# Four edits to a single-core attention and experts kernel: where the weights' low words are made, first matmuls on TensorE, when one block's keys and values are loaded, and where the bias tables come from

## The chip, the cores and the metric

The kernel runs on one core of a Trainium2 chip. The metric is the device time of one execution in microseconds (us), lower is better. The times are medians of several runs; beside them stands one execution that was profiled, with a time and a span of its own. Engines are named as the profile names them: PE (TensorE, matrix multiply), PEld (its weight loads), DVE (VectorE), ACT (ScalarE), POOL (GpSimd), SP (SyncE, which here only issues DMAs). PSUM is the memory that PE writes to, SBUF the working memory.

## The reference

Three layers follow one another, all in float32. There are 4 x 576 = 2304 tokens of width 512.

```python
# 1. attention, B, H, S, D = 4, 8, 576, 64, window 128
scores = np.matmul(q, k.transpose(0, 1, 3, 2)) / np.sqrt(D)
bias = slopes[:, None, None] * (-np.abs(rel))      # slopes[h] = 2.0 ** -(h + 1)
mask = (rel >= 0) & (rel < 128)
scores = np.where(mask, scores + bias, -1e9)
attn = softmax(scores)                              # row maximum taken off, sum + 1e-9
x = heads_joined(np.matmul(attn, v))                # (2304, 512)
# 2. dense layer, w_in 512 x 2048, w_out 2048 x 512
h = x @ w_in
x = (h - np.tanh(h)) @ w_out
# 3. eight experts, one per token
idx = argmax(normalised(x) @ normalised(expert_emb).T / tau)
out[idx == e] = gate * (np.maximum(x[idx == e] @ w1[e], 0) @ w2[e])
```

## The kernel before

Products that need float32 exactness are made of two words: a matrix is rounded to a high word (a cast, usually by ACT) and a low word (the matrix less its high word, a subtraction with two inputs by DVE or POOL), and PE multiplies high by high, high by low and low by high.

The work is cut into tasks. Each task has one engine, or a choice of engines with a cost for each (a dictionary such as `{"DVE": 0.72, "POOL": 1.32}`), a due time, and the things that it reads and writes. A planner (`Plan.order`) walks through the tasks with these costs: of the tasks that are ready it takes the one that can start first, and of those that can start together the one with the smallest due time. The order that comes out is the order of the instructions on each engine; the engines then run in order, and wait for each other only where data demand it. `port=True` tells the planner that such a task doesn't start on DVE while POOL is at work. SP's DMAs are one in-order queue: an issue that waits for its buffer holds all the issues behind it.

Attention goes over 18 blocks of 128 tokens, each in four quarters of two heads (`quarter`). In a quarter PE makes the scores (L485 in blocks 0 to 3, which use float32 keys and queries in one piece; L491 later, with two words, `khl` and `qst`). DVE adds the bias and takes the maximum (`soft`, L513), which reads the table `bias` of that head. ACT takes the exponential (`exp`, L527), PE transposes (`tr_pe`, L548), ACT or DVE copies the result out (L552), and PE multiplies it by the values (`pv_f`, L562). `x_out` transposes the finished block for the dense layer (L664, and L671 and L672 split it into words in `xT`). Blocks 0 and 1 have to be finished before the first step of the dense layer (`step`, L712 and L736) can start. The two score banks are reused: the next scores into a bank wait for the exponential that reads it.

The bias tables are made on the chip before: SP loads one float32 table (`tmp`, L251), and `consts` multiplies it by the slope of each head (L255), two heads on DVE and six on POOL; POOL also casts the triangle `tri` that the routing needs (L258).

Blocks 0 to 3 take keys and queries from their own loads (`qk_early`, L415 and L420). Block 4 needs the keys and values of block 3 also in the later form, so `qk_half` and `v_half` run for block 3 as well: SP loads `stk` (L375; one buffer, so the second half waits until the first is used) and `vst` (L443), ACT casts (L381), and POOL or DVE subtracts (L385).

The dense layer's weights (`weight`, L335 and on) are 32 loads of 512 KB that DVE and ACT unpack (L339, L342, L347, L351). After seven of the nine groups of two blocks, the routing (`route`) decides on the expert of each token: a chain of small DVE instructions (L826, L830, `chain` with L847 to L852) whose result `oh` PE multiplies by `tri` (`pos`, L862). In the same stretch the experts' weights begin to arrive: `e_weight` loads a piece of 128 x 512, ACT casts it (L1080) and DVE or POOL makes the low word (L1084). There are 128 such pieces. The experts' products are L1186, L1217, L1221 and, for one tile, L1306.

Of the kernel before, what the change touches and what calls it, by code (L numbers as in the profile page):

```python
# [10 lines left out]
F32 = mybir.dt.float32  # L11
F32R = mybir.dt.float32r
F16 = mybir.dt.float16
BF16 = mybir.dt.bfloat16
# [4 lines left out]
ALU = mybir.AluOpType  # L19
# [4 lines left out]
B, H, S, D = 4, 8, 576, 64  # L24
# [15 lines left out]
NF = 4  # L40
# [7 lines left out]
WLEAD2 = 6  # L48
N0 = 1
NPX = 16  # L50
NALT = 8
NOWN = 8
NXO = 2
# [2 lines left out]
QK = 2  # L56
# [122 lines left out]
class Builder:  # L179
# [61 lines left out]
    def zero(self, P):  # L241
        for n, t in enumerate(self.wz):
            P.add({"DVE": 0.6}, lambda e, t=t: self.nc.vector.memset(t, 0), -30, w=[("wz", n)])

    def consts(self, P):
        nc, i = self.nc, self.i
        at = {}

        def tmp(e):
            at[0] = self.at.tile([128, 512], F32, tag="xr", name="tmp", bufs=1)  # L250
            nc.sync.dma_start(out=at[0][:, 0:384], in_=i["c_bias"])  # L251

        P.add({"SP": 0.55}, tmp, -20, w=[("xr", m) for m in range(4)])
        for h in range(H):
            P.add({"DVE": 0.3} if h < 2 else {"POOL": 0.88}, lambda e, h=h: self.eng(e).tensor_scalar(  # L255
                out=self.bias[:, h, :], in0=at[0][:, 0:256], scalar1=2.0 ** -(h + 1), scalar2=None, op0=ALU.mult),
                -20 + h, r=[("xr", 0)], w=[("bias", h)])
        P.add({"POOL": 0.5}, lambda e: nc.gpsimd.tensor_copy(out=self.tri, in_=at[0][:, 256:384]), -11,  # L258
              r=[("xr", 0)], w=["tri"])

    def small(self):
        nc, i = self.nc, self.i
# [194 lines left out]
    def quarter(self, P, a, due):  # L457

        nc = self.nc
        b, qd = divmod(a, 4)  # L460
        hf, qq = divmod(qd, 2)
        s, n = b % 2, (2 * b + hf) % 2
# [9 lines left out]
        bank = "acc" if a < NALT and a % 2 else "sc"  # L472
# [141 lines left out]
        for jj in range(2):  # L614
            if early:
                P.add({"PE": 0.3 if one else 0.42}, lambda e, jj=jj: scores(jj), due,
                      r=["at", ("qf", b)] + [("kf", x) for x in ([b] if one else [b, b - 1])], w=[(bank, jj)])
            else:
                P.add({"PE": 0.13 if one else 0.24}, lambda e, jj=jj: scores(jj), due,
                      r=["at"] + ks + [("kl", x, hf) for x in kv] + q, w=[(bank, jj)])  # L620
        for jj in range(2):
            P.add({"DVE": ttr}, lambda e, jj=jj: soft(jj), due, r=["at", ("bias", qd * 2 + jj)],
                  w=[(bank, jj), ("mx", jj, a % 2)])
        for jj in range(2):
            P.add({"ACT": 0.49 if one else 0.64}, lambda e, jj=jj: exp(jj), due,
                  r=["at", (bank, jj), ("mx", jj, a % 2)], w=[("p32", pb, jj), ("sm", sk, qq, jj)])
        sm = [("sm", sk, x, y) for x in range(2) for y in range(2)]
        half = [("xr", 2 * hf), ("xr", 2 * hf + 1)]
        if early:
# [3 lines left out]
                  r=["at", ("tp", a)] + ([("h", own)] if own is not None else []), w=[("pt", a % 2)],  # L633
                  free="misc" if own is None else None)
            P.add({"PE": 0.45 if one else 0.9}, pv_f, due,
                  r=["at", ("pt", a % 2)] + [("vf", x) for x in ([b] if one else [b - 1, b])], w=[("o", qq)] if qq else ["o", ("o", 0), ("o", 1)])
            if qq:
# [4 lines left out]
              w=[("ph", a % 2)], port=True)  # L642
        P.add({"POOL": 0.84, "DVE": 0.46} if one else {"POOL": 1.19, "DVE": 0.71}, s_lo, due,
              r=["at", ("p32", pb, 0), ("p32", pb, 1), ("ph", a % 2)], w=[("ph", a % 2, 1)], port=True)
        P.add({"SP": 0.7 if one else 1.2}, tr, due, late=LATE, r=["at", ("ph", a % 2), ("ph", a % 2, 1)], w=[("pt", a % 2)])
        P.add({"PE": 0.28 if one else 0.56}, pv, due,
              r=["at", ("pt", a % 2)] + [("vt", x, hf, m) for x in kv for m in range(3)], w=["o"])
# [412 lines left out]
    def e_weight(self, P, e, kind, f, due):  # L1060

        nc, i = self.nc, self.i
        ff = f + FE // 128 * (e % 2)
        n = self.nld % NST
        self.nld += 1
        key, st = (kind, ff), ("est", n)
        v = {}
        w1, w2 = [i[w].rearrange("e k f -> (e k) f") for w in ("w1", "w2")]

        def load(_):  # L1070
            t = v["x"] = self.ex.tile([128, 512], F32, tag=f"est{n}", name="est")
            if kind == "i":
                half, k = divmod(f, KD)
                nc.sync.dma_start(out=t, in_=w1[bass.ds(self.at_row[e][0] + k * 128, 128), half * 512:(half + 1) * 512])
            else:
                nc.sync.dma_start(out=t, in_=w2[bass.ds(self.at_row[e][1] + f * 128, 128), :])

        def hi(_):
            t = self.w[key] = self.wp.tile([128, 2, 512], F32R, tag=f"w{kind}{ff}", name=f"e{kind}{ff}")
            nc.scalar.copy(out=t[:, 0, :], in_=v["x"])  # L1080

        def lo(eng):
            t = self.w[key]
            self.eng(eng).tensor_tensor(out=t[:, 1, :], in0=v["x"], in1=t[:, 0, :].bitcast(F32), op=ALU.subtract)  # L1084

        P.add({"SP": 0.73}, load, due - 4, r=["at", ("place", e)], w=[st], lag=LAG)
        P.add({"ACT": 0.65}, hi, due, r=[st], w=[(key, 0), (key, 1)])
        P.add({"DVE": 0.72, "POOL": 1.32}, lo, due, r=[st, (key, 0)], w=[(key, 1)], port=True)

    def e_rows(self, P, v, t, due):  # L1090

# [249 lines left out]
    def build(self):  # L1341
        tc, nc = self.tc, self.nc
        for n in ("kf", "qf", "vf", "sums", "oh4", "qst", "xr", "acc", "w"):
            setattr(self, n, {})
        self.setup()
        dp = self.pool("dr", bufs=1, space=DRAM, tilewait=False)
        self.bucket = dp.tile([ROWS, ROW], F32, name="bucket")
        self.pa = dp.tile([2 * N0, 128, DM], F32, name="pa")
        self.nw = 0
        self.sent, self.puts = [], []  # L1350
        P = Plan()
        P.add({"POOL": 2.7}, lambda e: self.small(), 0, w=["small", "cum"])
        self.zero(P)
        self.consts(P)
        self.small_loads(P, -19)
        all_f = list(range(FP))
        fa, fb = all_f[:FA], all_f[FA:]
        visits = ([(g, fa) for g in range(N0)] + [(N0, all_f)] + [(g, fb) for g in range(N0)]
                  + [(g, all_f) for g in range(N0 + 1, NG)])

        def weights(fps, due, rate):
            for x, fp in enumerate(fps):
                for kind in "io":
                    for f in (2 * fp, 2 * fp + 1):
                        self.weight(P, kind, f, due + x * rate + 1.2 * (kind == "o"))

        weights(fa, -WLEAD, WRATE)
        p, xi, seen = 0, 0, set()
        for g, fps in visits:
            sl = [xi % XR, (xi + 1) % XR]  # L1370
            xi += 2
            rate = RATE if g <= N0 else 1.0
            for n in range(2):
                b = 2 * g + n
                d0 = p - 8 * rate - (LEADM if g > N0 else LEAD) + 4 * n * rate
                if g not in seen:
                    for hf in range(2):
                        due = d0 + 2 * hf * rate
                        self.qk_half(P, b, hf, due - QK)
                        if b < NF and hf == 0:  # L1380
                            self.qk_early(P, b, due - QK - 2)
                            self.v_full(P, b, due)
                        if b >= NF - 1:
                            self.v_half(P, b, hf, due)
                        for qq in range(2):
                            self.quarter(P, 4 * b + 2 * hf + qq, due + qq * rate)
                if g not in seen:
                    self.x_out(P, b, sl[n], d0 + 4 * rate)
                    if b == 0:
                        self.emb(P, 0)  # L1390
            if g == N0:
                weights(fb, p + len(fa) - WLEAD2, WRATE2)
            for fp in fps:
                self.step(P, p, g, fp, sl, fp == fps[0], fp == fps[-1])
                for e in range(E):
                    if p == PAD + e // PADN:
                        self.pad(P, e, p)
                p += 1
            if g < N0 and g not in seen:
                self.spill(P, p - 1, g, sl)  # L1400
            else:
                if g == NG - 1:
                    self.moe2(P, p, lambda: self.route(P, g, sl, p))
                else:
                    self.route(P, g, sl, p + 1)
                if g == NG - 3:
                    self.choose(P, p + 2)
                    self.space(P, p + 2)
            seen.add(g)
        with tc.manual_schedule():  # L1410
            for fn, e in P.order({"misc": 1}):
                fn(e)
        self.overflow()
        while self.open:
            k = list(self.open)[-1]
            self.close(k)
# [140 lines left out]
def layout(inputs):  # L1557
    f = np.float32
# [6 lines left out]
    def tr(x):  # L1565
# [18 lines left out]
        "emb": np.ascontiguousarray(inputs["moe2_expert_emb"]),  # L1584
        "w1": np.ascontiguousarray(inputs["moe2_w1"]),
        "w2": np.ascontiguousarray(inputs["moe2_w2"]),
        "c_bias": np.concatenate([cur, prev, r < c], axis=1).astype(f),
        "c_con": np.concatenate([
            np.eye(128, dtype=f), row(np.arange(E, dtype=f) - E), row(np.arange(E, dtype=f) * NT),
            (np.arange(NB)[None, :] * 128 + r).astype(f), row(np.asarray(inputs["moe2_tau"]).reshape(1))], axis=1),  # L1590
# [16 lines left out]
```

## Time and profile before

| | |
|---|---|
| Median of 3 runs | 781.98 us (780.95 to 782.5) |
| Profiled execution, its own time | 785.27 us |
| Profiled execution, span from first to last instruction | 783.4 us |
| PE busy | 760.1 us, 97% of the span |
| DVE, ACT, POOL busy | 549.5, 427.9, 382.6 us |
| Mean granted clock of PE | 0.993 |

The span is told by the trace; the time of the execution is 1.9 us longer. Busy shares are averages over stages with different limits, and a busy PE need not be at its full rate, so the stages are read one by one.

### The profile page before, as it was taken

What the parts mean: (1) busy time and instruction counts of PE and PEld (TensorE: products, weight loads), DVE (VectorE), ACT (ScalarE), POOL (GpSimd) and SP (SyncE); (2) the same over time, 40 slices, a digit from 0 to 9 for tenths busy, and PEclk for the clock granted to TensorE, in tenths of its full rate; (3) what the DMA queues carried; (4) which work ended last, traced back from release to release, by engine and by line L of the source; (5) the groups of instructions that cost most, each with busy time, mean ns of one, the idle gap of its engine ahead of it and who ended that gap; (6) DMA issues with size and microseconds to landing.
All of it is one profiled execution on the core that took longest, in us unless ns stands there. A gap on an engine that the chain in (4) does not pass through costs nothing.

```text
span 783.4 us, 15248 instructions
## 1 busy us (share of the span) xinstructions
PE 760.1 (97%) x5189; PEld 678.7 (87%) x5189; DVE 549.5 (70%) x1454; ACT 427.9 (55%) x969; POOL 382.6 (49%) x378
## 2 busy tenths in 40 slices
PE   6998999999999999999999999989999999999996
PEld 4877899889998999989899998979879898888895
DVE  4888887888777688778777776887626678675420
ACT  4878776655565465555645643645235565555321
POOL 3226023674666165364744732687216577655411
PEclk9999999999999999999999999999999999999998
DMA  7996169966365353554454243764257879897100
GB/s 269 385 372 195 44 200 296 247 155 113 108 131 139 69 116 104 119 117 133 95 123 121 62 81 88 184 201 148 76 160 208 230 218 261 216 237 218 44 29 30
DMA packets 152454, 124.25 MB, mean 159 GB/s; under 512 B 115301, under 2 KB 119397, under 8 KB 152112
## 3 DMA queue, kind: packets, MB, share of 16 engines
q1 hardware_dynamic: 149344, 111.39, 53.5%
q0 software_dynamic: 3024, 11.82, 4.1%
q8 instruction: 42, 0.69, 0.4%
q14 instruction: 44, 0.36, 0.2%
HBM read 84.29 MB, written 22.06 MB: 136 GB/s over the span
## 4 chain that ended last, share of the span: by engine, by line
PE 87%; DVE 4%; issue 4%; ACT 2%; POOL 2%; DMA 1%; SPq 0%; POOLq 0%
PE h L712 25%; PE acc L736 23%; PE he L1186 12%; PE y L1221 10%; PE o L573 3%; PE sc L491 3%; PE y L1217 3%; PE of L562 2%; PE sc L485 1%; PE misc L548 1%; PE misc L664 1%; PE ht L1306 1%; DMA tmp<-in_c_bias 1%; PE misc L821 1%; DVE xA L1146 0%
## 5 line engine op out<-in xcount | busy, mean ns | idle before, releaser
L712 PE MATMUL h<-xT,wi 128*128 128x256 f32 x1728 | 227.8, 286 | 0.8 <-DVE xT L672 0.5
L712 PEld LDWEIGHTS h<-xT,wi 128*128 128x128 f32 x1728 | 219.7, 193 | 6.8 <-DVE xT L672 0.7
L736 PE MATMUL acc<-wo,gh 128*128 128x512 f32 x576 | 183.4, 400 | 0.4 <-DVE wo L351 0.4
L736 PEld LDWEIGHTS acc<-wo,gh 128*128 128x128 f32 x576 | 101.0, 190 | 16.6 <-issue 1.0
L736 PE MATMUL acc<-wo,gl 128*128 128x512 f32 x288 | 113.0, 392 | 0.0
L717 ACT ACTIVATE t<-h 128x512 f32<-128x512 f32 x72 | 43.0, 597 | 105.7 <-PE h L712 100.2
L1221 PE MATMUL y<-eo,ge 128*128 128x512 f32 x336 | 88.0, 398 | 0.2 <-ACT yo L1229 0.2
L527 ACT ACTIVATE p<-sc,mx 128x256 f32<-128x256 f32 (+1 forms) x128 | 59.0, 462 | 39.4 <-DVE mx L513 27.4
L1221 PEld LDWEIGHTS y<-eo,ge 128*128 128x128 f32 x336 | 60.1, 188 | 10.5 <-ACT yo L1229 0.4
L729 DVE TENSOR_TENSOR gl<-t,gh 128x512 fp32r<-128x512 f32 x72 | 64.4, 895 | 6.7 <-ACT gh L725 6.4
L537 POOL TENSOR_TENSOR ph<-p,ph 128x512 f16<-128x512 f32 (+1 forms) x37 | 43.9, 1187 | 51.1 <-ACT ph L532 40.5
L736 PEld LDWEIGHTS acc<-wo,gl 128*128 128x128 f32 x288 | 54.3, 189 | 12.2
L385 POOL TENSOR_TENSOR khl<-stk,khl 64x512 fp32r<-64x512 f32 x24 | 31.8, 1325 | 67.3 <-ACT khl L381 61.3
L720 DVE TENSOR_TENSOR t<-h,t 128x512 f32<-128x512 f32 x72 | 49.5, 687 | 18.5 <-ACT t L717 18.2
L1208 DVE SCALAR_TENSOR_TENSOR ge<-he,ge 128x256 fp32r<-128x256 f32 x104 | 28.8, 315 | 46.7 <-ACT ge L1202 46.3
L513 DVE CUSTOM_DVE_ANT_0 sc<-sc,bias 128x256 f32<-128x256 f32 (+1 forms) x136 | 49.6, 374 | 15.5 <-PE sc L491 9.5
L1246 POOL DMA_INDIRECT out<-yo,ix x23 | 25.0, 1089 | 69.9 <-ACT yo L1242 63.0
L1202 ACT ACTIVATE ge<-he 128x288 fp32r<-128x288 f32 (+2 forms) x56 | 23.2, 414 | 61.2 <-PE he L1186 42.5
L1186 PEld LDWEIGHTS he<-xA,ei 128*128 128x128 f32 x384 | 54.1, 189 | 2.6
L1186 PE MATMUL he<-xA,ei 128*128 128x288 f32 (+2 forms) x384 | 56.0, 296 | 0.0
L1186 PEld LDWEIGHTS he<-xT,ei 128*128 128x128 f32 x384 | 53.5, 188 | 2.2
L1186 PE MATMUL he<-xT,ei 128*128 128x288 f32 (+2 forms) x384 | 55.0, 295 | 0.0
(224 smaller groups left out, 1444.3 us busy)
## 6 DMA issues: line engine op xcount, KB each, us to landing
est<-in_w SPq DMA_DIRECT2D x128, 256.0 KB, 3.6
bucket<-in_c_pad SPq DMA_DIRECT2D x8, 1155.0 KB, 9.7
rawi<-in_w_in SPq DMA_DIRECT2D x16, 511.8 KB, 7.3
rawo<-in_w_out SPq DMA_DIRECT2D x16, 511.8 KB, 8.9
stk<-in_k SPq DMA_DIRECT2D x30, 256.0 KB, 2.8
stq<-in_q SPq DMA_DIRECT2D x28, 256.0 KB, 3.0
vst<-in_v SPq DMA_DIRECT2D x30, 128.0 KB, 2.8
xe<-bucket SPq DMA_DIRECT2D x3, 384.0 KB, 3.4
```

The source lines that it names most:

```text
L385: self.eng(e).tensor_tensor(out=k, in0=r4("k")[64:128], in1=k.bitcast(F32), op=ALU.subtract)
L513: nc.vector.tensor_tensor_reduce(out=x, in0=x, in1=self.bias[:, h, c0:c1], scale=-0.125, scalar=mx[:, 1:2] if m else 3.0e38, op0=ALU.add, ...
L527: nc.scalar.activation(out=v["p32"][:, jj * W:(jj + 1) * W], in_=x, func=AF.Exp, scale=-1.0, bias=v["mx"][jj][:, 0:1], accum_out=self.sums ...
L537: self.eng(e).tensor_tensor(out=ph[:, 2 * W:4 * W], in0=v["p32"][:, 0:2 * W], in1=ph[:, 0:2 * W], op=ALU.subtract)
L712: nc.tensor.matmul(h3(v["h"], f2), lhsT=w[:, a, k, :], rhs=xT[c][:, :, k, :], start=(k == 0 and n == 0), stop=(k == KD - 1 and n == 2))
L717: nc.scalar.activation(out=v["t"], in_=v["h"].rearrange("p a b -> p (a b)"), func=AF.Tanh)
L720: nc.vector.tensor_tensor(out=v["t"], in0=v["h"].rearrange("p a b -> p (a b)"), in1=v["t"], op=ALU.subtract)
L729: self.eng(e).tensor_tensor(out=v["gl"], in0=v["t"], in1=v["gh"].bitcast(F32), op=ALU.subtract)
L736: nc.tensor.matmul(self.acc[g, t], lhsT=v[a][:, c0:c0 + 128], rhs=self.w["o", fs[f2]][:, c, :], start=(first and f2 == 0 and n == 0), stop ...
L1186: nc.tensor.matmul(h[:, 0:N], lhsT=w[:, a, c0:c0 + 128], rhs=xT()[b][:, k, 0:N], start=(k == 0 and n == 0), stop=(k == KD - 1 and n == 2))
L1208: nc.vector.scalar_tensor_tensor(out=g[:, o:o + c1 - c0], in0=hk[f][:, c0:c1], scalar=0.0, in1=g[:, c0:c1].bitcast(F32), op0=ALU.max, op1= ...
L1221: nc.tensor.matmul(y[t], lhsT=gt(f, a)[:, (t - ts[0]) * 128:(t - ts[0] + 1) * 128], rhs=self.w["o", f0 + f][:, b, :], start=(f == 0 and n ...
```

## The change

Four things are changed.

- `warm` is new. DVE first fills a tile with ones, and PE multiplies it by itself (128 x 512, bfloat16, results not used): 7 times ahead of everything else, 8 times after the scores of quarter 0, and twice after those of quarters 1, 2 and 3. They write the PSUM bank `h0`.
- The bias tables of all eight heads are constants in bfloat16 (128 x 2048 and the triangle of 128 x 128), loaded by three DMAs of ACT's queue: heads 0 and 1, heads 2 to 7, the triangle. SP's load, the eight multiplications and the cast are gone.
- For block 3, the due times of `qk_half` and `v_half` are 3 later.
- The low words of the experts' weights (L1084 before) are made by DVE alone.

```diff
+WARM = [7, 8, 2, 2, 2]
+    def warm(self, P, n, due, r=()):
+        nc = self.nc
+        def run(e):
+            y = self.misc("h0")
+            for _ in range(n):
+                nc.tensor.matmul(y, lhsT=self.fill[:, 0:128], rhs=self.fill, start=True, stop=True)
+        def begin(e):
+            self.fill = self.m1.tile([128, 512], BF16, tag="gh0", name="fill", bufs=1)
+            nc.vector.memset(self.fill, 1.0)
+        if not r:
+            P.add({"DVE": 0.3}, begin, -40, w=[("gh", 0)])
+        P.add({"PE": 0.22 * n}, run, due, r=[("gh", 0), *r], w=[("h", 0)])
     def consts(self, P):
-            nc.sync.dma_start(out=at[0][:, 0:384], in_=i["c_bias"])
-        P.add({"SP": 0.55}, tmp, -20, w=[("xr", m) for m in range(4)])
-        for h in range(H):
-            P.add({"DVE": 0.3} if h < 2 else {"POOL": 0.88}, lambda e, h=h: self.eng(e).tensor_scalar(
-                out=self.bias[:, h, :], in0=at[0][:, 0:256], scalar1=2.0 ** -(h + 1), ...
-        P.add({"POOL": 0.5}, lambda e: nc.gpsimd.tensor_copy(out=self.tri, in_=at[0][:, 256:384]), -11, ...
+            nc.scalar.dma_start(out=self.bias[:, h0:h1, :],
+                                in_=i["c_bias"][:, h0 * 256:h1 * 256].rearrange("p (h t) -> p h t", h=h1 - h0))
+        for h0, h1 in ((0, 2), (2, H)):
+            P.add({"AQ": 3.0}, lambda e, h0=h0, h1=h1: table(e, h0, h1), -40, w=[("bias", h) for h in range(h0, h1)])
+        P.add({"AQ": 1.0}, lambda e: nc.scalar.dma_start(out=self.tri, in_=i["c_bias"][:, H * 256:]), -40, w=["tri"])
...
+        if a + 1 < len(WARM) and WARM[a + 1]:          # in quarter(), after the scores
+            self.warm(P, WARM[a + 1], -30, [(bank, 0), (bank, 1)])
...
-        P.add({"DVE": 0.72, "POOL": 1.32}, lo, due, r=[st, (key, 0)], w=[(key, 1)], port=True)
+        P.add({"DVE": 0.72}, lo, due, r=[st, (key, 0)], w=[(key, 1)], port=True)
...
+        self.warm(P, WARM[0], -40)
...
-                        self.qk_half(P, b, hf, due - QK)
+                        late = 3 if b == NF - 1 else 0
+                        self.qk_half(P, b, hf, due - QK + late)
...
-                            self.v_half(P, b, hf, due)
+                            self.v_half(P, b, hf, due + late)
```

## Rows read from the trace of the kernel before

**Rows 1.** The page: busy time by engine.

```profile
PE 760.1 (97%) x5189; PEld 678.7 (87%) x5189; DVE 549.5 (70%) x1454; ACT 427.9 (55%) x969; POOL 382.6 (49%) x378
```

**Rows 2.** PE's waits over the run: waited for, us, times, longest.

```profile
PE sc L485 <- DMA kf<-in_k: 4.2, 1, 4.2
PE misc L862 <- DVE oh L852: 3.6, 1, 3.6
PE sc L491 <- ACT p L527: 3.1, 3, 2.7
PE sc L485 <- ACT p L527: 2.3, 1, 2.3
```

**Rows 3.** Timeline, the first 7 us: start, us, engine, line, operation.

```profile
0.88 0.48 DVE L243 MEMSET xrow<- 128x512 int32 x1 [0.88 <-PEq L1599]
...
1.16 0.42 SPq L415 DMA_DIRECT2D kf<-in_k  x1
...
6.16 0.69 DVE L255 TENSOR_SCALAR bias<-tmp 128x256 bf16<-128x256 f32 x2 [4.25 <-DMA tmp<-in_c_bias]
6.22 5.48 POOL L255 TENSOR_SCALAR bias<-tmp 128x256 bf16<-128x256 f32 x6 [4.55 <-DMA tmp<-in_c_bias]
```

**Rows 4.** Timeline of PE, 8 to 22 us.

```profile
8.39 0.69 PE L548 MATMUL misc<-con,p 128*128 128x128 f32 x2
...
13.38 1.22 PE L562 MATMUL of<-vf,ptf 128*128 128x128 f32 x4
...
18.30 0.71 PE L562 MATMUL of<-vf,ptf 128*128 128x128 f32 x4
...
20.00 0.66 PE L548 MATMUL misc<-con,p32x 128*128 128x128 f32 x4
```

**Rows 5.** The chain that ended last, in order of time: start, us, work.

```profile
99.95 2.75 PE acc L736 x12
```

**Rows 6.** Stretches: length, busy PE, PEld, DVE, ACT, POOL; PEclk, DMA share, GB/s.

```profile
8.00:12.00 4.00, 4.00 (x16) 2.67 (x15) 1.72 (x10) 2.79 (x12) 3.70 (x6) 1.00 1.02 391
...
16.50:20.00 3.50, 3.50 (x20) 2.45 (x18) 2.34 (x13) 2.33 (x9) 1.27 (x1) 1.00 0.18 56
...
69.00:72.40 3.40, 3.02 (x14) 3.02 (x15) 3.18 (x9) 2.95 (x7) 1.93 (x2) 0.50 0.00 0
```

**Rows 7.** SP's queue, two neighbouring rows of its timeline.

```profile
8.41 1.78 SPq L335 DMA_DIRECT2D rawi<-in_w_in  x3
18.20 0.33 SPq L375 DMA_DIRECT2D stk<-in_k  x1
```

**Rows 8.** Stretches where the experts' weights arrive, columns as in rows 6.

```profile
500.00:510.00 10.00, 10.00 (x73) 9.02 (x72) 9.00 (x8) 7.17 (x13) 10.00 (x7) 1.00 0.52 140
510.00:520.00 10.00, 8.82 (x67) 7.85 (x65) 9.86 (x13) 5.56 (x10) 8.65 (x8) 1.00 0.76 236
...
523.00:526.40 3.40, 3.40 (x15) 3.11 (x14) 2.87 (x6) 1.10 (x2) 2.33 (x2) 0.51 0.55 178
...
640.00:680.00 40.00, 40.00 (x233) 35.62 (x232) 33.18 (x61) 24.25 (x46) 27.68 (x24) 1.00 0.82 230
```

**Rows 9.** The same for line 1084 alone: busy DVE, busy POOL.

```profile
500.00:510.00 10.00, 1.51 (x1) 8.03 (x5) 1.00 0.52 140
510.00:520.00 10.00, 3.53 (x3) 7.96 (x7) 1.00 0.76 236
...
640.00:680.00 40.00, 15.16 (x14) 14.97 (x12) 1.00 0.82 230
```

**Rows 10.** Timeline of DVE, 499 to 530 us.

```profile
499.85 1.65 DVE L1084 TENSOR_TENSOR ei<-est,ei 128x512 fp32r<-128x512 f32 x1
...
519.91 1.19 DVE L849 TENSOR_TENSOR lg<-lg,rs 128x16 f32<-128x16 f32 x1
...
521.02 0.16 DVE L850 TENSOR_TENSOR eq<-eq,con 128x16 f32<-128x16 f32 x1
...
529.90 0.69 DVE L1084 TENSOR_TENSOR eo<-est,eo 128x512 fp32r<-128x512 f32 x1
```

More of the change, by code (lines that the diff above doesn't have):

```diff
@@ L243, in zero, with table @@
             P.add({"DVE": 0.6}, lambda e, t=t: self.nc.vector.memset(t, 0), -30, w=[("wz", n)])
+    def warm(self, P, n, due, r=()):
[10 more added lines that the diff above has]
+        P.add({"PE": 0.22 * n}, run, due, r=[("gh", 0), *r], w=[("h", 0)])
     def consts(self, P):
         nc, i = self.nc, self.i
-        at = {}
-        def tmp(e):
-            at[0] = self.at.tile([128, 512], F32, tag="xr", name="tmp", bufs=1)
-            nc.sync.dma_start(out=at[0][:, 0:384], in_=i["c_bias"])
-        P.add({"SP": 0.55}, tmp, -20, w=[("xr", m) for m in range(4)])
-        for h in range(H):
-            P.add({"DVE": 0.3} if h < 2 else {"POOL": 0.88}, lambda e, h=h: self.eng(e).tensor_scalar(
[L256 to L259, printed above, removed]
+        def table(e, h0, h1):
+            nc.scalar.dma_start(out=self.bias[:, h0:h1, :],
[3 more added lines that the diff above has]
+        P.add({"AQ": 1.0}, lambda e: nc.scalar.dma_start(out=self.tri, in_=i["c_bias"][:, H * 256:]), -40, w=["tri"])
     def small(self):
@@ L1586, in layout @@
         "w2": np.ascontiguousarray(inputs["moe2_w2"]),
-        "c_bias": np.concatenate([cur, prev, r < c], axis=1).astype(f),
+        "c_bias": np.concatenate([np.concatenate([cur, prev], axis=1) * 2.0 ** -(h + 1) for h in range(H)] + [r < c],
+                                 axis=1).astype(mybir.dt.np(BF16)),
         "c_con": np.concatenate([
```

## The prediction

> **What bounds the kernel now.** I read the page first, then PE's waits, then the stages in which PE waits or runs slowly. PE is busy for 760.1 of 783.4 us [rows 1], so nearly every stage is PE's, and what can be won is PE's idle time and its time at a low rate. The waits show where: 4.2 us for the first keys, 2.3 us behind the first scores, 2.7 us at 65.5 us, and 3.6 us for `oh` in the routing [rows 2]; the rest is small, but for the tail behind the last product, which no edit touches.
>
> At the start two things hold PE up. The first bias is multiplied at 6.16 us, though the first scores could start at 4.2, and POOL needs until 11.7 for the other heads [rows 2, 3]. And PE is slow: four value products take 1.22 us at 13.38 and 0.71 us at 18.30, two transposes 0.69 us at 8.39 and four 0.66 us at 20.00 [rows 4]. The granted clock reads 1.00 there, but I go by the durations: until about 17 us PE is at 1.2 GHz, after that at 2.4. In mid-run the chain is PE without a gap, 12 products of 512 columns in 2.75 us, 0.23 each [rows 5].
>
> The first load stage is DMA's: its engines are full at 8 us (1.02), yet 0.18 busy from 16.5 to 20 [rows 6]. SP's queue shows why: after the issues that end at 10.2 it stands until 18.20 on a load of `stk`, which is block 3's keys [rows 7]. That is 3.5 x 0.82 = 2.9 us of empty DMA.
>
> In the routing DVE is the bound: 9.00 and 9.86 of 10 us [rows 8]. In the same 20 us POOL makes 12 low words of the experts' weights, 16.0 us of work [rows 9]. DVE's two-input instructions are long there: 1.65 us for a low word and 1.19 for 16 columns, against 0.69 for a low word at 529.90 and 0.16 for 16 columns at 521.02 [rows 10]. They wait for POOL.
>
> **The change, part by part.**
>
> *Bias by ACT's queue.* Removed: eight multiplications and a cast, with 5.48 us on POOL and 0.69 on DVE [rows 3]; POOL has nothing else then, so its part counts only through the heads that were late. Added: three issues on ACT, each taken at the 0.42 us of an SP issue [rows 3]; ACT has no arithmetic before 7 us, so they are hidden, and without that cover they would cost 1.3. The tables are 544 KB instead of 192 KB: 352 KB more, 0.9 us at the 391 GB/s of [rows 6]. The keys were issued at 1.16 and are there at 4.2 [rows 2, 3]; the tables issued at about 0.7 should be there between 4 and 5, a gain of 1.2 to 2.2 us for the first soft step, if they don't hold up the keys, which costs at most 544 KB / 391 = 1.4.
>
> *Ones first.* The fill is a DVE memset, done by 1.4 us if it takes the 0.48 of its neighbour [rows 3]. A warm product isn't in the trace; by the nearest row it is 0.23 us at the upper level [rows 5], so 0.46 at the lower. The first 7 end at 1.4 + 3.2 = 4.6, into the 4.2 us wait: 0.4 late. Quarter 0's scores take some 0.6. The next 8 stand in PE's in-order queue ahead of quarter 1's scores and quarter 0's transposes, which wait for them; 2.3 us of them fall into an idle stretch. They take 1.8 us at the upper level, 3.7 at the lower, then 0.6 for scores and two more ones. The transposes, now at 8.39, come at 4.6 + 0.3 + 1.8 + 0.3 + 0.5 = 7.5 if the clock is up by 4.6, at 4.6 + 0.6 + 2.8 + 0.6 + 0.5 = 9.1 if it rises half-way through the 8, at 4.6 + 0.6 + 3.7 + 0.6 + 0.9 = 10.4 if not. From there to the products at 18.30 it takes 9.9 us now, about 8.2 at the lower level. At the upper one that is 8.2 x 0.71/1.22 + 1.7 = 6.5, plus two pairs of ones 0.9: 7.4. So the mark comes at 14.9, 16.5 or, with the clock low as long as now (9.9 + 1.8 behind 10.4), 22.1: a gain of 3.4 or 1.8, or a loss of 3.8. The nearest row decides: after 3.4 us of nearly unbroken products at 0.50, PE was granted full speed at 72.4 [rows 6]. That is the middle case: **1.8 us**.
>
> The rows also show that a busy PE alone doesn't bring the level up: 4.00 of 4.00 us busy from 8 to 12 [rows 6], at the slow durations. The Trainium skill, "TensorE: Matmul & The Clock Gate", section Part 1, says that the low clock is the default and sustained matmul activity releases it. By that alone the clock would have been up by 12 us before, against the rows; for the bursts of ones it gives the middle case, 1.8.
>
> *Block 3 later.* Eight loads and casts and their subtractions move behind some of the dense weights; the first use of `khl` is at 60 us, so nothing waits for them. SP's queue no longer stands at 10 us, so the 2.9 us hole is filled, less 0.9 for the tables: the weights come 2.0 us earlier. PE doesn't wait for them before 57 us, so the gain by itself is nothing; but it lets the 1.8 of the start pass through the stage up to 70 us, where DVE unpacks weights as they land. Bounds: 0 of the 1.8 kept, or the 2.7 wait at 65.5 and the half clock behind it (3.4 x 0.50 = 1.7) gone too.
>
> The Trainium skill, "DMA: Bandwidth & Descriptors", section "Issuing engines are not separate DMA queues", says that issuing from another engine saves only issue time, as all queues share the engines. By it the tables hold up the keys by the whole 1.4 us, and the start is worth 0.4 instead of 1.8; no row here shows two queues side by side.
>
> *Low words by DVE.* In 500 to 520 us DVE runs 20 instructions, 12 of 512 columns and 8 small. Unhindered they would be 12 x 0.69 + 8 x 0.16 = 9.6 us, against 18.9 now [rows 8, 10]: 9.3 come back when POOL is still. The 12 low words cost 12 x 0.69 = 8.3. So if all stood ahead of `oh`, it would come 1 us earlier; if few do, the small chain alone (four steps of about 1.2, each cut to 0.16) gives 4. Bounds: 0, or the 3.6 wait and the half clock behind it, 3.4 x 0.49 = 1.7 [rows 2, 8], together 5.3. Some 1.3 us of low words stay ahead: **4.0 us**. POOL's other two-input work still hinders DVE.
>
> Later, DVE is at 33.2 of 40 us in its fullest stretch [rows 8]. Twelve more low words add 8.3; its own 14 return 15.16 - 14 x 0.69 = 5.5 [rows 9]. At 36 of 40 PE still has its weights in time; without that return DVE would need 41.5 and cost 1.5.
>
> **Sum:** 785.27 - 1.8 - 4.0 = 779.5 for the profiled execution. It stands 0.42% above the median, so 779.5 x 781.98 / 785.27 = **776.2 us**.
>
> **Rivals.**
> - *The wait at 65.5 goes too.* For it: the empty DMA before it is filled. Against: DVE and ACT are full there whatever loads. 2.7 + 1.7 more: about 771.5. Chance 0.17.
> - *Little arrives.* The clock rises late, or PE comes earlier to a DVE stage that ends when it did, or `oh` comes only 1 us earlier: one of the two terms is lost, or both: 778 to 782. For it: the rows of a busy, slow PE. Chance 0.23.
> - *DVE becomes the bound in the routing.* If the 12 low words go ahead of `oh` and the 9.3 don't come back, because POOL's joins and casts keep hindering DVE, the wait grows by 8.3: 781.98 - 1.8 + 8.3 = 788.5. It decides once less than 8.3 - 1.8 = 6.5 of the 9.3 returns. Against: 16.0 of POOL's 18.7 us there are the low words. Chance 0.12.
>
> **Numbers.** The forecast has 0.48: 774 to 778.5 by its own bounds. 0.2% is 1.6 us, about what a measurement of this kernel can tell from no change. Faster: 0.48 + 0.17 + half of 0.23 = 0.77; the other half of the third case is split, 0.10 the same and the rest slower with the last case, 0.13. The range reaches down to the first rival and up to the end of the second, 770 to 782.5.
>
> **What would show it.** Transposes of quarter 0 at 9 us and short from then on; no hole in the DMA share at 17 us; DVE's low words at 0.69 us and small steps at 0.16 near 520 us; no 3.6 us wait for `oh` and no half clock there. The prediction is wrong if PE's pace at 10 to 17 us is still slow, if `oh` is as late, or if the planner's new order makes a new wait of several us.

## The result and the profile after

The changed kernel takes 773.5 us (median of 6 runs, 771.67 to 777.16), against 781.78 us of the kernel before on the same chip (6 runs, 780.49 to 784.95). The ratio is 0.9896 with a 95% interval of 0.9876 to 0.9915: 1% faster, inside the range of the forecast and 2.7 us below its middle. The profiled execution took 773.47 us with a span of 771.7, 11.7 us less than the span of before; the medians differ by 8.3, since the execution of before that was profiled is slower than any of those six.

The page, busy time by engine (against [rows 1]):

```profile
PE 758.0 (98%) x5210; PEld 673.9 (87%) x5210; DVE 548.5 (71%) x1498; ACT 430.3 (56%) x971; POOL 306.1 (40%) x324
```

PE does 21 products of ones more and is still busy for 2 us less: it ran fast for more of the time. POOL lost 76.5 us and DVE gained nothing, though it took over POOL's low words. PE's waits of the whole run, the longest four (waited for, us, times, longest):

```profile
PE misc L253 <- DVE fill L257: 1.4, 1, 1.4
PE misc L835 <- DVE xT L686: 1.4, 1, 1.4
PE sc L497 <- DMA kf<-in_k: 1.1, 1, 1.1
PE h L726 <- DVE t L734: 1.0, 1, 1.0
```

The three long waits of [rows 2] are gone: behind the first scores, at 65.5 us and for `oh`. Where they stood, PE goes on. Timeline of PE at the start (start, us, engine, line, operation; L497 are scores, L560 transposes, L574 value products, L253 ones):

```profile
1.43 3.17 PE L253 MATMUL misc<-fill 128*128 128x512 bf16 x7 [1.43 <-DVE fill L257]
5.65 0.80 PE L497 MATMUL sc<-kf,qf 64*128 64x128 f32 x4 [1.05 <-DMA kf<-in_k]
6.38 3.60 PE L253 MATMUL misc<-fill 128*128 128x512 bf16 x8
9.90 0.80 PE L497 MATMUL scx<-kf,qf 64*128 64x128 f32 x4
10.63 0.60 PE L253 MATMUL misc<-fill 128*128 128x512 bf16 x2
...
11.58 0.44 PE L560 MATMUL misc<-con,p 128*128 128x128 f32 x2
...
12.81 0.61 PE L574 MATMUL of<-vf,ptf 128*128 128x128 f32 x4
```

The keys, which PE had at 4.15 us before, come at 5.65. The ones take 0.45 us each in both bursts, the pace of the lower level; at 10.6 us it changes, and the two transposes at 11.58 take 0.44 us where before they took 0.69, the four value products 0.61 where before they took 1.22 [rows 4]. The transposes of quarter 0 come 3.2 us later than before, and all behind them runs at the upper level. The trace's own records of the granted clock begin with a step up to full speed, at 10.6 us here and at 17.8 in the kernel before, which bears out the reading by durations: the 1.00 shown ahead of that step is no measurement. Stretches (length; busy PE, PEld, DVE, ACT, POOL; granted clock, DMA share, GB/s), against [rows 6, 8]:

```profile
16.00:20.00 4.00, 4.00 (x28) 2.81 (x27) 3.58 (x18) 3.22 (x12) 0.00 (x0) 1.00 1.04 410
500.00:510.00 10.00, 10.00 (x88) 9.21 (x87) 8.22 (x16) 5.53 (x11) 0.40 (x1) 1.00 0.89 228
510.00:520.00 10.00, 10.00 (x71) 9.19 (x70) 8.53 (x29) 5.23 (x11) 2.15 (x3) 1.00 0.63 207
640.00:680.00 40.00, 39.77 (x234) 35.44 (x233) 28.30 (x67) 22.38 (x43) 12.74 (x11) 1.00 0.90 242
```

The hole in the DMA at 17 us is filled: 1.04 instead of 0.18. In the routing POOL is nearly still, and DVE runs 44 instructions in 16.75 us where before it ran 20 in 18.86 (one that crosses 510 us stands in both rows). Timeline of DVE there (against [rows 10]):

```profile
509.40 0.68 DVE L1098 TENSOR_TENSOR eo<-est,eo 128x512 fp32r<-128x512 f32 x1
...
510.80 0.18 DVE L862 TENSOR_TENSOR eq<-lg,rs 128x16 f32<-128x16 f32 x1
```

A low word takes 0.68 us and a small step 0.18, as in the undisturbed rows of before.

For the rest, four marks are read from each trace: the transposes that finish block 0 and block 3 (L664 before, L678 here), the product with `oh` near 520 us (the eighth of nine in the run, the one that PE waited 3.6 us for before), and the end of the span. Each kernel's times in us:

| kernel | block 0 | block 3 | `oh` | end |
|---|---|---|---|---|
| before | 20.50 | 64.71 | 522.40 | 783.4 |
| after | 20.02 | 62.65 | 512.98 | 771.7 |
| e1 low words alone | 19.43 | 64.23 | 519.12 | 779.4 |
| e10 late loads alone | 20.29 | 63.80 | 522.84 | 784.3 |
| e9 ones alone | 16.96 | 61.99 | 520.12 | 779.8 |
| e7 bias tables alone | 23.81 | 72.64 | 525.70 | 785.6 |
| e6 ones and tables | 18.67 | 63.49 | 519.01 | 778.7 |
| e2 after, low words undone | 19.17 | 61.80 | 513.35 | 772.9 |
| e3 after, ones undone | 26.60 | 74.57 | 529.92 | 788.2 |
| e4 after, late loads undone | 18.69 | 63.53 | 518.24 | 777.6 |
| e5 after, tables undone | 17.73 | 61.84 | 513.27 | 771.7 |
| e11 first ones only | 26.56 | 74.53 | 533.90 | 794.0 |
| e8 nine and four ones | 16.37 | 58.89 | 517.89 | 781.0 |
| e12 most tables by SP | 17.71 | 65.33 | 519.67 | 781.4 |

They are marks of one execution each, and two of the profiled executions are far from typical: that of e9 lies 4.3 us above the median of e9 and that of e8 4.5 us above the median of e8, the slowest of each. The start also moves from run to run. The kernel before and e1 have the same order of instructions on every engine up to about 500 us, and so have the changed kernel and e2 up to about 495; yet block 0 ends 1.1 us earlier in e1 and 0.85 in e2, where the level rose earlier (16.2 against 17.8 us, 8.8 against 10.6). So leads of under 1 us in this table say little, and the comparisons go by the medians. By the marks the changed kernel is 2.1 us ahead at block 3, 9.4 at `oh` and 11.7 at the end. Between the first two lie 2.7 us of wait and 3.4 x 0.50 = 1.7 of half clock that are gone at 65 to 72 us [rows 2, 6], less a new wait of 1.0, and the 3.6 us for `oh`: 7.0 of 7.3. Between the last two lies the half clock at 523 [rows 8], 1.7 of 2.3.

### The profile page after: what moved, and what is told of

It reads as the page before. It is cut to its first block, busy times and chain, and to the rows that moved or that the text cites. A ratio compares the mean times of both kernels' runs of the same rounds, so it can differ in the third digit from the quotient of the medians.

```text
span 771.7 us, 15216 instructions
## 1 busy us (share of the span) xinstructions
PE 758.0 (98%) x5210; PEld 673.9 (87%) x5210; DVE 548.5 (71%) x1498; ACT 430.3 (56%) x971; POOL 306.1 (40%) x324
## 4 chain that ended last, share of the span: by engine, by line
PE 90%; issue 3%; DVE 3%; DMA 1%; ACT 1%; POOL 1%; SPq 0%; POOLq 0%; ACTq 0%; DVEq 0%
PE h L726 26%; PE acc L750 24%; PE he L1200 11%; PE y L1235 10%; PE o L585 4%; PE sc L503 3%; PE y L1231 3%; PE of L574 2%; PE sc L497 1%; PE misc L678 1%; PE misc L560 1%; PE ht L1320 1%; DMA est<-in_w 1%; PE misc L253 1%; PE misc L835 1%
## 5 line engine op out<-in xcount | busy, mean ns | idle before, releaser
L726 PEld LDWEIGHTS h<-xT,wi 128*128 128x128 f32 x1728 | 217.2, 191 | 6.4 <-DVE t L734 1.2
L549 POOL TENSOR_TENSOR ph<-p,ph 128x512 f16<-128x512 f32 (+1 forms) x39 | 45.8, 1175 | 60.4 <-ACT ph L544 44.9
L743 DVE TENSOR_TENSOR gl<-t,gh 128x512 fp32r<-128x512 f32 x72 | 61.6, 855 | 6.0 <-ACT gh L739 5.7
L734 DVE TENSOR_TENSOR t<-h,t 128x512 f32<-128x512 f32 x72 | 49.4, 686 | 16.4 <-ACT t L731 16.2
L397 POOL TENSOR_TENSOR khl<-stk,khl 64x512 fp32r<-64x512 f32 x25 | 33.9, 1356 | 52.8 <-ACT khl L393 50.6
L1098 DVE TENSOR_TENSOR eo<-est,eo 128x512 fp32r<-128x512 f32 x64 | 50.9, 795 | 5.2 <-ACT eo L1094 5.2
```

Source lines behind the costliest of these rows:

```text
L397: self.eng(e).tensor_tensor(out=k, in0=r4("k")[64:128], in1=k.bitcast(F32), op=ALU.subtract)
L549: self.eng(e).tensor_tensor(out=ph[:, 2 * W:4 * W], in0=v["p32"][:, 0:2 * W], in1=ph[:, 0:2 * W], op=ALU.subtract)
L726: nc.tensor.matmul(h3(v["h"], f2), lhsT=w[:, a, k, :], rhs=xT[c][:, :, k, :], start=(k == 0 and n == 0), stop=(k == KD - 1 and n == 2))
L734: nc.vector.tensor_tensor(out=v["t"], in0=v["h"].rearrange("p a b -> p (a b)"), in1=v["t"], op=ALU.subtract)
L743: self.eng(e).tensor_tensor(out=v["gl"], in0=v["t"], in1=v["gh"].bitcast(F32), op=ALU.subtract)
```

## The experiments

Four kernels undo one edit of the changed kernel, four make one edit alone, one makes two, and three vary the start. Each was timed against the kernel before on the same chip.

**e1, low words alone.** The kernel before, with

```diff
-        P.add({"DVE": 0.72, "POOL": 1.32}, lo, due, r=[st, (key, 0)], w=[(key, 1)], port=True)
+        P.add({"DVE": 0.72}, lo, due, r=[st, (key, 0)], w=[(key, 1)], port=True)
```

> The kernel before with one part of the change: the experts' low words by DVE alone. Theory A (POOL's low words hold up DVE's two-input instructions, and that is the 3.6 us wait for oh): the wait for oh and the half clock behind it are gone, low words take 0.69 us near 510 us, the first 80 us are as before, and the time falls by 4 to 5.5 us, to about 777. Rival B (any new plan would have moved that wait; the hold-up isn't its cause): small steps of the routing get short but PE waits elsewhere, and the time stays within 1.5 us of 781.8.

Measured: 779.78 us, ratio 0.996 (0.9943 to 0.9976). Timeline of DVE near the routing in e1:

```profile
517.65 0.17 DVE L848 TENSOR_TENSOR eq<-lg,rs 128x16 f32<-128x16 f32 x1
517.86 0.18 DVE L849 TENSOR_TENSOR lg<-lg,rs 128x16 f32<-128x16 f32 x1
```

The steps are short and no wait for `oh` is left: the mechanism is shown. In the profile e1 is 3.3 us ahead at `oh` and 4.0 at the end; the medians give 2.8, less than the 4 to 5.5 expected. The routing itself gave more. From the seventh product with `oh` to the ninth it takes 86.0 us before (470.3 to 556.4) and 80.7 in e1: 5.3 less, the wait and the half clock together. The same stretch takes 80.7 us in all eight kernels here whose low words are made by DVE alone, whatever else they change.

**e2, low words undone.** The changed kernel with the line of e1 turned back.

> The changed kernel with one part undone: low words of the experts by DVE or POOL again. Theory A: POOL is full again near 500 us, DVE's two-input instructions take 1.2 to 1.7 us there, PE waits 3 to 4 us for oh, the clock halves behind it, and the time rises by 4 to 5.5 us to about 778. Rival B: the order of the new plan avoids the wait with POOL's work too; within 1.5 us of 773.5.

Measured: 774.99 us, ratio 0.9896 (0.9867 to 0.9924), the ratio of the changed kernel. Undone in this order of the work, the edit costs nothing that the times can tell. The trace has a small part of it: the stretch from the seventh to the ninth product with `oh` takes 83.0 us in e2, 2.2 more than in the changed kernel and 3.1 less than before. A stretch of e2, columns as above:

```profile
500.00:510.00 10.00, 10.00 (x85) 9.08 (x85) 9.83 (x10) 6.12 (x11) 10.00 (x8) 1.00 0.90 204
```

The timeline of DVE, POOL and PE in e2, in order of time:

```profile
507.68 1.76 DVE L1098 TENSOR_TENSOR ei<-est,ei 128x512 fp32r<-128x512 f32 x1
...
509.57 2.98 POOL L1098 TENSOR_TENSOR ei<-est,ei 128x512 fp32r<-128x512 f32 x2
...
512.04 0.55 DVE L862 TENSOR_TENSOR eq<-lg,rs 128x16 f32<-128x16 f32 x1
...
512.62 0.18 DVE L863 TENSOR_TENSOR lg<-lg,rs 128x16 f32<-128x16 f32 x1
...
513.17 2.99 POOL L1098 TENSOR_TENSOR eo<-est,eo 128x512 fp32r<-128x512 f32 x2 [0.62 <-ACT eo L1094]
...
513.35 0.18 PE L876 MATMUL misc<-oh,tri 128*128 128x8 bf16 x1 [0.87 <-DVE oh L866]
```

POOL is full again and a low word of DVE takes 1.76 us. But POOL stands from 512.55 to 513.17, for want of a cast of ACT's, and just there a small step runs at 0.18. PE waits 0.87 us instead of 3.6, and no half clock follows. The Trainium skill, "SBUF — State Buffer", section "Who interferes with whom", says that a VectorE instruction with two SBUF inputs contends with a GpSimd instruction that reads SBUF, and that whichever was issued first holds the ports. This trace agrees: 1.76 us beside POOL's low words, 0.18 for a small step in POOL's gap. What such a chain costs thus depends on how it meets POOL's work. In the other kernels that leave the low words as they were, the wait for `oh` is 0.9 (e6), 1.1 (e7), 2.1 (e9) and 1.4 us (e10): any of the other edits shortened it, so the 3.6 of before was an unlucky meeting.

**e3, ones undone.** The changed kernel with

```diff
-WARM = [7, 8, 2, 2, 2]
+WARM = []
-        self.warm(P, WARM[0], -40)
```

> The changed kernel without the products of ones. Theory A (the ones bring the clock up by 10.6 us, and that is the lead at 20 to 30 us): the value products at 10 to 16 us take 1.2 us for four again, the transposes of the first finished block come 1 to 2 us later than 20.0, the time rises by 1.5 us to 775. Rival C (the constants for the bias alone make the lead; the 8 ones hold up quarter 0's transposes by over 3 us for nothing): same or up to 1.5 us faster, 772 to 773.5.

Measured: 789.96 us, ratio 1.0088 (1.0061 to 1.0115): without the ones the other three edits make the kernel slower than before. Timeline of PE in e3, and then a stretch:

```profile
9.46 1.22 PE L574 MATMUL of<-vf,ptf 128*128 128x128 f32 x4
...
23.44 1.22 PE L574 MATMUL of<-vf,ptf 128*128 128x128 f32 x4
...
27.28 1.95 PE L574 MATMUL of<-vf,ptf 128*128 128x128 f32 x16
```

```profile
20.00:24.00 4.00, 4.00 (x11) 2.27 (x11) 0.83 (x3) 1.40 (x4) 0.00 (x0) 1.00 1.03 405
```

Four value products take 1.22 us until 23.4 and 16 take 1.95 at 27.3. PE is at 1.2 GHz until 27 us, by the durations (the granted clock reads 1.00 all along; its first record, a step to full speed, is at 27.0), although it is busy for 4.00 of 4.00 us from 8 us on. Block 0 ends 6.6 us later than in the changed kernel and block 3 11.9 later. The loss is 15 us by the ratios (1.9%) and 16.5 by the medians and the spans, ten times what was expected.

**e4, late loads undone.** The changed kernel with

```diff
-                        late = 3 if b == NF - 1 else 0
+                        late = 0
```

> The changed kernel with block 3's keys and values as early as before. Theory A (SP's queue stands on stk, the DMA engines run empty, DVE unpacks later and PE waits at 65 us): a hole in the DMA share between 13 and 20 us, dense weights 2 us later, PE waits of 2 to 5 us between 55 and 75 us, time up by 2 to 5 us to 776 to 778. Rival D (the hole is harmless, the wait at 65 us left because the plan's order there is another): DMA hole but no new wait, within 1.5 us of 773.5.

Measured: 779.61 us, ratio 0.9957 (0.9936 to 0.9979); the edit is worth 0.6% here. Timeline of SP's queue in e4, and then stretches:

```profile
8.41 1.86 SPq L347 DMA_DIRECT2D rawi<-in_w_in  x3
15.00 0.33 SPq L387 DMA_DIRECT2D stk<-in_k  x1
```

```profile
64.00:68.00 4.00, 2.42 (x13) 1.99 (x12) 3.78 (x10) 3.61 (x7) 0.00 (x0) 0.85 0.63 205
68.00:72.00 4.00, 4.00 (x28) 4.00 (x27) 3.78 (x9) 2.90 (x8) 2.25 (x2) 0.72 0.14 41
```

SP's queue stands again, for 4.7 us, PE is idle for 1.6 of 4 us from 64 us, and a half clock follows. Near 181 us PE waits 1.8 us more for POOL (L678 for `xr`), which it doesn't in the changed kernel. By `oh` e4 is 5.3 us behind, of the 5.9 between the spans.

**e5, bias tables undone.** The changed kernel with the eight multiplications and the cast of before in place of the three loads by ACT.

> The changed kernel with one part undone: the bias tables are made on the chip from SP's one float32 table again. Theory A (the constants are worth little once the ones stand in PE's queue until about 10 us, and their 544 KB delay the first keys from 4.2 to 5.6 us): first keys at 4.2 to 4.5 us, first bias at 6.2 us, POOL's tables done before quarter 2 needs them, time within 1.5 us of 773.5. Rival C (the constants make the lead at 20 us): the first transposes of a finished block 1 to 2 us later, 775 to 776.

Measured: 775.88 us, ratio 0.9923 (0.9909 to 0.9938). The profiled execution, the quickest of its six, has the span of the changed kernel, 771.7; the medians say that the tables as constants are worth some 0.3%, and the intervals just overlap. Timeline of PE in e5 (L503 are scores, L566 transposes):

```profile
4.52 0.80 PE L503 MATMUL sc<-kf,qf 64*128 64x128 f32 x4
...
9.51 0.44 PE L566 MATMUL misc<-con,p 128*128 128x128 f32 x2
```

Without the tables on ACT's queue the keys are there when the first burst ends, at 4.52, and the transposes come 2.1 us earlier. Block 0 ends 2.3 us earlier, block 3 only 0.8, and by `oh` the lead is gone.

**e7, e9 and e10, one edit alone.** The kernel before with the three loads of tables (e7), with the ones (e9), with the later due times of block 3 (e10).

> The kernel before with the bias constants alone. Theory A (they bring the first soft step no earlier, as they delay the first keys to 5.6 us, and the clock stays low): first keys at 5.6 us, four value products take 1.2 us until 17 us or longer, time 782 to 788, not faster. Rival C (the constants make the lead of the start): 1 to 2 us faster, 780 to 781.

> The kernel before with the products of ones alone. Theory A (they bring the clock up by 9 to 11 us): value products at 0.6 to 0.7 us for four from 12 us on, lead of 1 to 2 us at 20 to 30 us, and then the waits at 65 us and in the routing as the plan has them: 776 to 781. Rival E (the ones need the early bias: without it PE stands behind them and POOL's tables come too late): no lead at 20 us, 781 to 784.

> The kernel before with block 3's loads later as the only edit. Theory A (SP's hole alone doesn't hold PE up before 57 us, since PE at the low clock is later than the weights; only the unpacking by DVE near 65 us may gain): DMA hole at 17 to 20 us gone, the same start, time 778 to 782. Rival F (the later loads are the gain in the changed kernel, whatever the start): 775 or less.

Measured: tables 788.49 us, ratio 1.0086 (1.0072 to 1.01); ones 777.41, 0.9931 (0.9918 to 0.9944); late loads 783.24, 1.0031 (1.0011 to 1.0051). Timeline of PE in e7 (L479 scores, L556 value products), then in e9 (L503 scores, L253 ones, L566 transposes):

```profile
5.22 0.80 PE L479 MATMUL sc<-kf,qf 64*128 64x128 f32 x4 [5.22 <-DMA kf<-in_k]
...
26.86 3.64 PE L556 MATMUL of<-vf,ptf 128*128 128x128 f32 x16
30.43 0.70 PE L479 MATMUL scx<-kf,qf 64*128 64x256 f32 x2
```

```profile
4.52 0.51 PE L503 MATMUL sc<-kf,qf 64*128 64x128 f32 x4
4.97 1.90 PE L253 MATMUL misc<-fill 128*128 128x512 bf16 x8
...
8.17 0.44 PE L566 MATMUL misc<-con,p 128*128 128x128 f32 x2
```

In e7 the keys come 1.1 us later than before, and 16 value products take 3.64 us at 26.86 where e3 has 1.95 at 27.3: PE is slow until about 30 us. In e9 the scores behind the first burst take 0.51 us where the changed kernel has 0.80, and the second burst 0.24 us a product: PE is fast from 4.6 us, where the first burst ends, and block 0 ends 3.5 us earlier than before. In e10 the hole is filled (a DMA share of 1.04 from 16.5 to 20 us) and nothing is won: the wait of PE for ACT stays, 2.56 us at 67.25, with a half clock.

**e6, ones and tables.** The kernel before with both.

> The kernel before with the ones and the bias constants alone. Theory A (without the later loads the dense weights come late and PE waits at 65 us as it did without that part; in the routing, POOL's low words can hit the small steps or miss them): lead of 1 to 1.5 us at 20 to 30 us, a wait of 1 to 4 us near 65 us; 778 to 781, and 5 us less only if both waits happen to miss. Rival D (the start alone makes the gain): 774 to 776.

Measured: 781.85 us, ratio 1.0001 (0.9989 to 1.0013). Two edits of which one alone loses 0.9% and the other wins 0.7% come out even. With the late loads they make e2, 1% faster: the edit that by itself was worth nothing or less is worth a full per cent on top of these two.

**e11, first ones only.** The changed kernel with

```diff
-WARM = [7, 8, 2, 2, 2]
+WARM = [7, 0, 0, 0, 0]
```

> The changed kernel with the first 7 ones alone, none behind the scores. If the first burst brings the clock up: upper level before 10 us, the transposes of quarter 0 near 8 us, 2 us earlier than in the changed kernel, 771 to 773. If it doesn't: the clock stays low as it does without any ones, until 25 us or later, and the time is 785 to 790.

Measured: 794.79 us, ratio 1.0157 (1.0134 to 1.0181). Stretches of e11:

```profile
24.00:27.00 3.00, 3.00 (x13) 2.02 (x13) 1.88 (x8) 1.02 (x4) 0.00 (x0) 1.00 1.02 407
27.00:30.00 3.00, 3.00 (x28) 2.83 (x26) 2.48 (x10) 1.81 (x6) 0.00 (x0) 1.00 1.04 400
```

Thirteen products in 3 us, then 28: the level rises at 27 us, as without any ones. So in the changed kernel the second burst and the pairs behind it are needed. That they would do it without the first burst is not shown, and in e9 the level was up when the first burst ended, ahead of the second. The time is beyond the 785 to 790 expected, and 0.7% above e3. That loss is not at the start: the order of instructions on PE, DVE, ACT and POOL is the same as in e3 but for the 7 ones, and block 3 is done at 74.5 us in both. It comes between 80 and 210 us, where PE waits 3.3 us for the DMAs of `pt` (0.9 in e3) and a half clock follows at 170 us; why these DMAs came later stays open.

**e8, nine and four.** The changed kernel with `WARM = [9, 4, 2, 2, 2]`: more ones while PE waits for the keys, fewer ahead of quarter 0.

> The changed kernel with 9 ones ahead of everything and 4 instead of 8 behind quarter 0's scores. The 8 stand at the lower level in front of quarter 0's transposes (11.58 us, though their input is ready at 7.7). If their number is what delays the start: transposes at 9.5 to 10 us, lead at 20 us 1 to 1.5 us more, time 772 to 773. If the clock needs them: it rises after 11 us, four value products take 1.2 us again for a while, and the time is 774 to 779.

Measured: 778.37 us, ratio 0.9951 (0.9935 to 0.9968): slower than the changed kernel, by 4.9 us. Neither theory fits, as the level rose early and the time did not fall. The profile is of the slowest of its 12 executions, 782.84 us, so the waits below need not be those of a typical one. Timeline of PE in e8, then PE's waits, then a stretch:

```profile
5.62 0.49 PE L497 MATMUL sc<-kf,qf 64*128 64x128 f32 x4 [0.35 <-DMA kf<-in_k]
...
8.38 0.44 PE L560 MATMUL misc<-con,p 128*128 128x128 f32 x2
...
62.66 0.55 PE L503 MATMUL sc<-khl,qst 128*128 128x256 f32 x2 [2.71 <-ACT p L539]
75.17 0.51 PE L503 MATMUL sc<-khl,qst 128*128 128x256 f32 x2 [3.78 <-ACT p L539]
```

```profile
PE sc L503 <- ACT p L539: 6.5, 2, 3.8
PE y L1235 <- ACT yo L1256: 2.4, 1, 2.4
```

```profile
670.50:674.00 3.50, 3.50 (x11) 2.77 (x11) 3.15 (x7) 3.42 (x7) 3.03 (x4) 0.51 0.97 244
```

The start is what the prediction had hoped for: fast from 5 us (as in e9 with 7 ones, so that the nine are the cause is not shown), transposes at 8.38, block 3 done 3.8 us ahead of the changed kernel. Then PE waits twice for ACT's exponentials, 6.5 us in all, and at 668 us 2.4 us for an output copy, with half clock behind them. The lead over the changed kernel is a lag of 4.9 us at `oh` and of 9.3 at the end.

**e12, most tables by SP.** The changed kernel with the load of heads 2 to 7 on SP's queue, behind the first keys and queries.

```diff
-            nc.scalar.dma_start(out=self.bias[:, h0:h1, :],
+            (nc.scalar if h0 == 0 else nc.sync).dma_start(out=self.bias[:, h0:h1, :],
-            P.add({"AQ": 3.0}, ..., -40, ...)
+            P.add({"AQ": 3.0} if h0 == 0 else {"SP": 1.1}, ..., -40 if h0 == 0 else -20, ...)
```

> The changed kernel with the tables of heads 2 to 7 (384 of the 544 KB) loaded by SP's queue behind the first queries and keys, instead of by ACT's at the same time. If the tables beside them delay the first keys: keys at 4.2 to 4.7 us instead of 5.65, scores and all behind them up to 1 us earlier at 20 us, time 772 to 773.5. If they don't: keys at 5.6 as before, same time.

Measured: 782.6 us, ratio 1.0002 (0.9986 to 1.0018). Timeline of PE at the start of e12, and then PE's waits:

```profile
4.93 0.80 PE L497 MATMUL sc<-kf,qf 64*128 64x128 f32 x4 [0.34 <-DMA kf<-in_k]
```

```profile
PE acc L750 <- DVE wo L363: 3.2, 3, 1.6
...
PE sc L503 <- ACT p L539: 1.8, 1, 1.8
```

The time is 9 us above what was expected for earlier keys. They do come 0.7 us earlier and block 0 ends 2.3 us earlier, as meant. Then PE waits 3.2 us for unpacked weights and 1.8 for an exponential, and block 3 ends 2.7 us later than in the changed kernel. No version here beats the changed kernel.

## Why the prediction was right, and where its steps were not

**The sum.** Forecast were 1.8 us at the start and 4.0 in the routing, 5.8 on the profiled execution. Its gain is 11.8 (785.27 less 773.47). By the accounting above: 2.1 at the start instead of 1.8; 3.4 at 65 to 72 us, which was the first rival with a chance of 0.17; 5.3 in the routing, the upper bound of the term; the rest, about 1, in small waits. The medians differ by 8.3 only, between the forecast's 5.8 and this. What the quicker executions of before lack of the 11.8 no trace shows. The record has their mean granted clock, mostly 0.995 or 0.996 against 0.993 for the profiled one: by estimate 783 x 0.002 to 0.003 = 1.6 to 2.3 us, about one half clock less.

So the time lies in the range and in the direction forecast, but not in the case that had the chance of 0.48: 773.5 is below its bounds of 774 to 778.5 and nearer to the first rival, whose own sum is 776.2 - 4.4 = 771.8 (the prediction says 771.5). That the number was close is in part luck: the prediction left the wait at 65.5 us standing and took less than the routing gave, and its price of the start held by another road.

**The start: the size came out right, by another road.** The first burst ends at 4.60, as worked out. From there the steps differ. The tables on ACT's queue hold up the keys by 1.5 us, which the prediction had as a bound and left at nothing; the Trainium skill's rule that it set against that ("DMA: Bandwidth & Descriptors", section "Issuing engines are not separate DMA queues") agrees, with the 1.4 that it gave: e5 has the scores at 4.52, e12 at 4.93, the changed kernel at 5.65. The 8 ones run wholly at the lower level, 3.6 us, and quarter 0's transposes come at 11.58: later than even the late case, 10.4 (in e2, where the level rose within the 8, at 10.74). What made good for it is the pace behind: from those transposes to the end of block 0 it takes 8.4 us instead of 12.1. At the mark that the prediction chose nothing was won: the value products of 18.30 come at 18.36, not at 16.5. The 2.1 us show only behind it, in block 3, and e2 has 2.9 by the same start.

**What the ones are worth was mis-sized.** The sum took the clock of before, fast from about 17 us, as what the kernel would have without them. But the edit of the tables changes that: e7, with the tables alone, is slow until 30 us and loses 0.9%, and e3 without the ones until 27. So the ones are worth 5 us in the kernel of before (e9) and 15 to 16.5 in the changed one (e3), and the prediction, which costed the tables at a gain of 1.2 to 2.2 us for the first soft step, had them wrong in sign when they stand alone. Why the level rose at 17 us before and at 27 to 30 in e3 and e7, the runs don't settle; what they show as a difference is that before PE stood for 2.3 us behind the first scores [rows 2] and e3 and e7 for 0.47. The spread from run to run doesn't look like the reason: with the start of before the level rose at 17.8, 16.2 (e1) and 18.8 us (e10), with that of e3 and e11 at 27.0 twice.

**Block 3's loads: the bound that was not taken.** The DMA hole is filled, as predicted. That it is worth nothing by itself is right too (e10, if anything slower). But the two bounds given, 0 and 2.7 + 1.7, were weighed by how full DVE and ACT are at 65 us, and that didn't decide: in the changed kernel DVE is busy for 3.78 and ACT for 3.91 of 4 us from 64 us, and PE for 3.89. With ones, tables and late loads together (e2 and the changed kernel) the wait went; without the late loads (e6, e4) or the tables (e5) a part of it and a half clock stayed.

**The routing: right mechanism, but not additive.** e1 shows the term: 5.3 us in the routing itself, the upper bound, of which 4.0 are left at the end of the profile and 2.8 by the medians, against 4.0 forecast. As the last edit (e2) it is worth nothing by the ratios, 1.2 us between the spans and 2.2 in the stretch itself: in the new order the small steps happen to fall into a gap of POOL's. So of the 5.3 us that are gone there, 3.1 would have gone without this edit. The prediction took one order of the work as given for all of its terms.

**DVE as the bound.** This rival didn't come. In 640 to 680 us the prediction had DVE rise from 33.2 to 36 us; it fell to 28.30. Line 1098 alone, busy DVE in that stretch of the changed kernel:

```profile
640.00:680.00 40.00, 19.40 (x27) 1.00 0.90 242
```

27 low words take 19.40 us, 0.72 each as costed. The other DVE work fell from 33.18 - 15.16 = 18.0 us in 47 instructions [rows 8, 9] to 8.9 in 40, 0.38 to 0.22 each. Its share of the waiting for POOL had been left out; that this is all of the fall is not shown, as the two stretches don't hold the same work.

**Parts and whole.** The four edits alone give -0.4, -0.7, +0.9 and +0.3%, together 0.1% slower; the whole is 1% faster. What ties them is the stretch from 60 to 80 us. A lead at the start counts only as far as the order that the planner makes there lets it through: block 3 is finished 2.1 us ahead in the changed kernel, which keeps this to the end, and 5.8 us ahead in e8, which has lost 1.3 of it by `oh`, although its wait for `oh` is gone too, and 3.4 by the end. The order does differ: PE's products leave the order of the changed kernel at 15.7 us in e5 and e12 and at 17.9 in e4 and e8. Where it stays the same, a lead that came with the run was kept once and lost once: e2 is 0.85 us ahead of the changed kernel at block 0 and still 0.6 at 464 us, while e1 is 1.1 ahead of before at block 0 and 0.5 behind at 470, with a half clock of 6.8 us at 67 us instead of 3.4. So that the order is what eats the leads of e8 and e12 is argued, not shown.

## What to carry to other kernels

Where a planner orders the work, test an edit both alone and as the last one taken out: here the late loads cost 0.3% alone and brought 0.6% in company, and the low words brought 0.4% alone and nothing that the times can tell as the last. Time the stretch that an edit works on between two marks on either side of it, too: that showed 5.3 and 2.2 us where the whole time showed 2.8 and nothing. Read the rate of the first products from their durations, and check in the trace that a warm-up did raise it; half of one can be worth nothing (e11). A lead won early is only worth what the next tight stage lets through, so look there for new waits before counting it.

## What the runs showed of the hardware

- PE that is busy without a gap can stay at 1.2 GHz for a long time: until 27 us in e3 and e11 and 30 us in e7, with scores, transposes and value products in float32. The Trainium skill, "TensorE: Matmul & The Clock Gate", section Part 1, has sustained matmul activity release the clock; by that rule these starts should have been fast much earlier, and the measurements decide against it for these products; which of the three kinds keeps the level low no run separates. With both bursts of bfloat16 ones the rise came between 4.6 us (e9) and 10.6 us (the changed kernel), and with one and the same start at 8.8 (e2) and 10.6.
- A product of ones of 512 columns took 0.45 us at the lower level (7 in 3.17) and 0.24 at the upper (8 in 1.90).
- Behind waits of PE of 2.7 to 3.8 us in mid-run came stretches at half clock (before at 69 and 523 us [rows 6, 8], e8 from 63 and from 77 us), of 3.4 us each and in e1 of 6.8; behind the wait of 1.0 us at 73 us in the changed kernel came none. Between these it went both ways: a half clock behind 1.4 us at 63 us in e5, none behind 1.8 us at 181 us in e4.
